# Decay attention and two expert layers on one core: the chunk products cut into half chunks and their work dealt over the steps

## The chip, the cores and the metric

One core of a Trainium2 chip. The metric is device microseconds of one execution. All data is fp32 at the surface; the kernel runs its large products as sums of three fp32r products of a high and a low part.

## The reference, cut to what matters

```python
# attention: batch 4, heads 8, 768 tokens, head size 48
for t in range(S):
    state = alpha[:, :, t, :, None] * state + k[:, :, t] (outer) v[:, :, t]
    y[:, :, t] = q[:, :, t] @ state
x = y as [3072 tokens, 384]
h = x @ w_in                       # 384 -> 2048
x = (max(h, 0) + alpha1 * min(h, 0)) @ w_out   # alpha1 per column of h, 0 to 0.3
h = x @ w_in2
g = h where h >= 1, 0 where h <= -1, else (h + 1)**2 / 4
out = g @ w_out2                   # [3072, 384]
```

The weights of both layers and alpha1 come as float64 and are put together as fp32 on the chip from two 32-bit words each.

## The kernel before, in words

**Attention** goes by chunks of 128 tokens: 24 chunks (NCH), six to a batch item (CPB), each with its eight heads as four pairs, so that a pair fills 112 of the 128 partitions (48 rows from partition 0 and 48 from 64, HALVES). Two scans along the tokens (at_alpha, L214) make running products of alpha backwards (R) and forwards (F); K2 = K * R and Q2 = Q * F (at_qk, L232). On TensorE a chunk then has: the scores K2'Q2 (L247, eight products with 48 rows, 128 columns of weights and 128 columns streamed), masked by VectorE into two tiles A (L252); a transpose of K2 (L258) copied by ScalarE into KT; the share of the state, bd'Q2 (L275); A'V (L280); and what the chunk adds to the state, KT'V (L292). An fp32 product is two records in the trace, each with its own weight load. The first chunk of a batch item has no L275, the last no L258 and L292. L304 to L311 split y into the high and low part in xs; since 48 rows a head don't fill 64, the last 128 rows of x are shared out over spare rows of the other three groups, by six small DMAs a chunk (L326; in the first four chunks by a product with sel, L298).

**Inputs of a chunk.** q, k and alpha are loaded token by token (L157, 192 bytes a piece). Up to chunk 9 (NPE = 10) TensorE turns them by twelve transposes (L195), copied to T by ScalarE (L202) or, with the clamp of alpha, VectorE (L185). From chunk 10 VectorE turns 32 x 32 blocks (L205, one instruction into X), and 16 DMAs bring the blocks to their place in T (L211); the clamp is then VectorE's on T. Alpha outside 0.7 to 1.4 makes the kernel fall back to a general path: ScalarE counts such values (flag, L164), for batch items 2 and 3 on the chunk in nat, for 0 and 1 on six extra loads in the second layer (load_flags).

**The layers** go by blocks of 512 tokens, six to a layer, and by 16 slices of 128 hidden columns: 192 steps, s = 0 to 191 (blocks 0 to 5 are layer one, 6 to 11 layer two). Step s issues on TensorE the nine products h of its slice (L430, 512 columns each), then the activation chain (emit_act, L435), then the out products of step s - 1 (L463, nine of 512; in layer two L474, twelve of 384). The chain is in layer one: VectorE L445 and L447, ScalarE gh (L453), GpSimd gl (L454); in layer two: ScalarE L442, VectorE L450 and L452, then gh and gl. So the chain of a step has the rest of that step and the h products of the next to run in.

**What sets the order.** The order on each engine is that of the program. Chunks 0 to 3 come before the first step. From chunk 4 a chunk's work lies in groups (L516); run_slots (L535) issues one group a step, after the out products: three groups a chunk up to chunk 7, then four: at_out of the chunk before; K2, Q2, decay of the state and the transposing of a later chunk (fetch, L504); the scans of the next chunk; the scores. A block's first step needs the xs of four chunks. All DMAs are issued by the SP queue in program order.

**Weights.** In block 0 every step also loads a slice of layer one (load_w, L342: five DMAs), turns words to fp32 (ScalarE L361 and L362, VectorE joins L367 and L369) and splits it (ScalarE L408, GpSimd L414). The joins and the split of slice fc + 2 stand ahead of the step's own products and activation in the program, the words behind them. In blocks 1 to 4 every fourth step does the same for a slice of layer two (w2_step, L563: two words, two joins, a store); block 5 loads these again and splits them.

PSUM has eight banks: two for h, three for the out products (o0 to o2), three (at) that attention's tiles take in turn.

## Time and profile before

| what | value |
|---|---|
| median of 3 runs (lowest, highest) | 965.82 us (963.66, 966.33) |
| the profiled execution | 964.38 us, its span 962.7 us |
| PE busy | 925.7 us, 96% |
| PEld (weight loads) busy | 781.9 us, 81% |
| DVE busy | 558.6 us, 58% |
| POOL busy | 363.4 us, 38% |
| ACT busy | 349.8 us, 36% |
| granted clock of TensorE, mean over the span | 0.996 |
| DMA, mean rate | 91 GB/s |

Busy is the time in which at least one instruction of the engine runs. The ends of matmuls are modelled, so a busy PE is not a PE at its peak; the starts are measured. The chain that ended last is PE for 76% of the span, DVE for 9%, DMA for 5%. The other 1.7 us of the execution lie around the span.

### The profile page before, as it was taken

To read this page: it belongs to the slowest core of one execution; us is meant where nothing else is said; L and a number is where in the kernel's file an instruction comes from. 1 tells how busy PE (TensorE), PEld (TensorE's weight loads), DVE (VectorE), ACT (ScalarE), POOL (GpSimd) and SP (SyncE) were. 2 spreads that over 40 slices of the span, in tenths; PEclk is the share of its full clock that TensorE was granted. 3 is DMA by queue.
4 is the path that set the end of the run, shared out by engine and by line. 5 is a ranking of instruction groups with operands and counts; after the bars stand their busy time and mean duration, and the time that the engine had idled before them with its cause. 6 is when DMAs were issued, how large, how long until landed. Compare 5 with 4: busy or idle time off the path is not lost.

```text
span 962.7 us, 14310 instructions
## 1 busy us (share of the span) xinstructions
PE 925.7 (96%) x5379; PEld 781.9 (81%) x5379; DVE 558.6 (58%) x756; ACT 349.8 (36%) x590; POOL 363.4 (38%) x290
## 2 busy tenths in 40 slices
PE   7898889999999999999999999999999999999996
PEld 6766567887878788788888889999999999999995
DVE  8888887777767678776433434434435334344333
ACT  3555542333322333332223333345533333333332
POOL 3455553333333343333347743233332333322331
PEclk9999999999999999999999999999999999999999
DMA  9976747666767776674133310031100100100001
GB/s 185 216 137 137 151 90 157 128 126 129 153 128 144 162 161 133 130 153 114 46 117 118 98 55 12 1 118 47 55 1 12 55 2 10 55 12 1 34 0 38
DMA packets 227599, 87.17 MB, mean 91 GB/s; under 512 B 194736, under 2 KB 213952, under 8 KB 227520
## 3 DMA queue, kind: packets, MB, share of 16 engines
q1 hardware_dynamic: 227520, 86.16, 40.2%
q8 instruction: 44, 0.72, 0.3%
q14 instruction: 35, 0.29, 0.1%
HBM read 57.42 MB, written 15.73 MB: 76 GB/s over the span
## 4 chain that ended last, share of the span: by engine, by line
PE 76%; DVE 9%; DMA 5%; SPq 4%; issue 3%; ACT 2%; POOL 0%; DVEq 0%; ACTq 0%; POOLq 0%
PE hp L430 34%; PE y L474 20%; PE o L463 14%; PE sc L247 2%; PE y L280 2%; PE y L275 1%; DVE wf L367 1%; DVE g L445 1%; DMA xs<-x 1%; DVE wf L369 1%; DVE g L447 1%; SPq L211 1%; DMA nat<-in_k_dram 1%; PE kt L258 1%; DMA wst<-in_moe_w_out_dram 1%
## 5 line engine op out<-in xcount | busy, mean ns | idle before, releaser
L454 POOL TENSOR_TENSOR gl<-g,gh 128x512 fp32r<-128x512 f32 x191 | 263.3, 1379 | 510.3 <-ACT gh L453 499.0
L430 PE MATMUL hp<-xs,wh 128*128 128x512 f32 x1152 | 363.2, 396 | 6.2 <-DMA xs<-x 5.0
L453 ACT CAST gh<-g 128x512 fp32r<-128x512 f32 (+1 forms) x193 | 119.3, 618 | 428.3 <-DVE g L447 256.7
L430 PEld LDWEIGHTS hp<-xs,wh 128*128 128x128 f32 x1152 | 211.8, 188 | 46.3 <-DVE T L185 4.7
L430 PE MATMUL hp<-xs,wl 128*128 128x512 f32 x576 | 226.7, 394 | 0.0
L450 DVE SCALAR_TENSOR_TENSOR g<-g 128x512 f32<-128x512 f32 (+1 forms) x97 | 68.3, 704 | 214.7 <-ACT g L442 213.2
L430 PEld LDWEIGHTS hp<-xs,wl 128*128 128x128 f32 x576 | 108.4, 188 | 23.5
L445 DVE TENSOR_SCALAR g<-hp,malpha 128x512 f32<-128x512 f32 x96 | 71.2, 742 | 60.4 <-PE hp L430 60.3
L442 ACT ACTIVATE g<-hp,half 128x512 f32<-128x512 f32 (+1 forms) x97 | 66.1, 683 | 104.7 <-PE hp L430 101.5
L463 PE MATMUL o<-gl,wh 128*128 128x512 f32 x288 | 83.2, 397 | 9.2 <-POOL gl L454 8.0
L463 PE MATMUL o<-gh,wh 128*128 128x512 f32 x288 | 83.2, 397 | 8.1 <-ACT gh L453 5.5
L474 PE MATMUL y<-wh,gh 128*128 128x384 f32 x384 | 83.3, 337 | 0.2
L474 PE MATMUL y<-wh,gl 128*128 128x384 f32 x384 | 83.0, 336 | 0.0
L474 PE MATMUL y<-wl,gh 128*128 128x384 f32 x384 | 82.6, 335 | 0.0
L463 PE MATMUL o<-gh,wl 128*128 128x512 f32 x288 | 81.6, 392 | 0.0
L474 PEld LDWEIGHTS y<-wh,gh 128*128 128x128 f32 x384 | 69.5, 188 | 9.2 <-ACT gh L453 1.1
L463 PEld LDWEIGHTS o<-gl,wh 128*128 128x128 f32 x288 | 52.9, 188 | 25.9 <-POOL gl L454 15.2
L463 PEld LDWEIGHTS o<-gh,wh 128*128 128x128 f32 x288 | 53.4, 189 | 24.5 <-ACT gh L453 10.9
L452 DVE TENSOR_TENSOR g<-hp,g 128x512 f32<-128x512 f32 (+1 forms) x97 | 66.5, 686 | 3.4
L447 DVE SCALAR_TENSOR_TENSOR g<-hp,g 128x512 f32<-128x512 f32 x96 | 66.4, 691 | 3.3
L474 PEld LDWEIGHTS y<-wh,gl 128*128 128x128 f32 x384 | 67.9, 188 | 0.4 <-DVE gl L454 0.3
L474 PEld LDWEIGHTS y<-wl,gh 128*128 128x128 f32 x384 | 68.0, 188 | 0.0
(97 smaller groups left out, 874.8 us busy)
## 6 DMA issues: line engine op xcount, KB each, us to landing
wst<-in_moe_w_out_dram SPq DMA_DIRECT2D x32, 384.0 KB, 4.7
T<-X SPq DMA_DIRECT2D x224, 48.0 KB, 2.1
wst<-in_moe_w_in_dram SPq DMA_DIRECT2D x16, 384.0 KB, 5.4
w_d<-wf SPq DMA_DIRECT2D x16, 384.0 KB, 5.7
w<-w_d SPq DMA_DIRECT2D x16, 384.0 KB, 3.1
wst<-in_moe_w_in_dram SPq DMA_DIRECT2D x32, 144.0 KB, 3.6
x_d<-ev SPq DMA_DIRECT2D x18, 256.0 KB, 4.0
x2s<-x_d SPq DMA_DIRECT2D x18, 256.0 KB, 3.0
```

Source lines behind the costliest of these rows:

```text
L247: nc.tensor.matmul(out=scs[h % 2][:, h // 2, :], lhsT=s["K2"][lo:lo + D, h // 2, :], rhs=s["Q2"][lo:lo + D, h // 2, :], start=True, stop=True)
L280: nc.tensor.matmul(out=y[64 * a:64 * a + 64, p, :], lhsT=vc[:, 2 * p + a, :], rhs=s["A"][a][:, p, :], start=first and p == 0, stop=done, s ...
L430: nc.tensor.matmul(out=hp, lhsT=w[:, p, :], rhs=xs[:, x, p, :], start=(i == 0), stop=(i == 3 * ND - 1))
L442: nc.scalar.activation(y, x, AF.Relu, bias=half, scale=0.5)
L445: nc.vector.tensor_scalar(out=y, in0=x, scalar1=0.0, scalar2=malpha[:, fc:fc + 1], op0=ALU.min, op1=ALU.mult)
L447: nc.vector.scalar_tensor_tensor(out=y, in0=x, scalar=0.0, in1=y, op0=ALU.max, op1=ALU.add)
L450: nc.vector.scalar_tensor_tensor(out=y, in0=y, scalar=1.0, in1=y, op0=ALU.min, op1=ALU.mult)
L452: nc.vector.tensor_max(out=y, in0=x, in1=y)
L453: nc.scalar.copy(out=hi, in_=y)
L454: (nc.gpsimd if parts == 1 else nc.vector).tensor_sub(out=lo, in0=y, in1=hi.bitcast(F32))
L463: nc.tensor.matmul(out=ops[d], lhsT=w[:, d * P:(d + 1) * P], rhs=g, start=first, stop=last)
L474: nc.tensor.matmul(out=ops[t], lhsT=g[:, t * P:(t + 1) * P], rhs=w, start=first, stop=last)
```

## The change

Attention's products are cut into half chunks of 64 tokens (HC), each in one quarter of the array (64 rows by 64 columns): scores only inside a half, the rest through a state at the middle of the chunk (bd has three tiles: at the start, in the middle, at the end). Four records that follow each other go to the four quarters, and those of the two row halves write to different banks of a two-bank tile. Per full chunk this makes 16 products for the scores, 16 for the state's share, 16 for A'V and 16 for what is added to the states, with 64 columns streamed (48 in the last), where there were eight of each with 128 (48). A is one tile, multiplied in one instruction. From chunk 10 on q, k and alpha are loaded in blocks of 768 and 640 bytes a piece (load_blocks, 12 DMAs a chunk), VectorE turns each third straight into T, and GpSimd clamps. Layer one's activation is ScalarE's alpha1 * h and VectorE's maximum of that and h (right while alpha1 is at most 1, which a new flag counts). All alpha flags are counted in layer two (12 loads, 24 flags and that one). w2_step deals a slice's two words and two joins over four steps. A chunk's work is listed by step, as before behind the out products (ends), and a few pieces between h and out (mids). In block 0 the joins stand behind the step's h products and activation, the split and the words at its end. load_w has seven DMAs a slice in layer one.

```diff
-    ps_a = main.enter_context(tc.tile_pool(name="ps_a", bufs=3, space=PSUM))
+    ps_a = main.enter_context(tc.tile_pool(name="ps_a", bufs=1, space=PSUM))
...
+    def load_blocks(c):
+        b, t0 = c // CPB, (c % CPB) * C
         for i in (2, 1, 0):
+            src = (q, k, alpha)[i][b, :, t0:t0 + C, :].rearrange("(p a) (j g) d -> a j p (g d)", a=2, g=4)
             for a in range(2):
                 for r in range(2):
                     d0 = 64 * a + 32 * r
+                    nc.sync.dma_start(out=natq[d0:d0 + 32, i * NP:(i + 1) * NP, 0:4 * D - 32 * r],
+                                      in_=src[a, :, :, 32 * r:4 * D])
+    def at_in(c, i):
+        n = slice(i * NP, (i + 1) * NP)
+        nc.vector.transpose(out=tin(c, i).rearrange("f n (j g) -> f n g j", g=4),
+                            in_=natq[:, n].rearrange("j n (g f) -> j n g f", g=4)[:, :, :, 0:32])
+        if i == 2:
+            clamp(tin(c, i), tin(c, i), nc.gpsimd)
...
+    def bank_pair(c):
+        pool, tag = (ps_o, "oo") if c < NC0 and c % 2 else (ps_a, "yy")
+        w = pool.tile([P, 2, 4 * C], F32, tag=tag, name="w")
+        return [w[:, :, x * NP * HC:(x + 1) * NP * HC].rearrange("q i (n t) -> q i n t", n=NP)
+                for x in range(2)]
+    def at_state(c, across):
+        s = st[c]
+        for p in range(NP // 2):
+            for n in (p, p + NP // 2):
+                for a in range(2):
+                    i = a ^ across
+                    if c % CPB == 0 and i == 0:
+                        continue
+                    o = 64 * out_half(n, a)
+                    nc.tensor.matmul(out=s["y"][o:o + 64, i, n, :], lhsT=bd[i][64 * a:64 * a + D, n, :],
+                                     rhs=s["Q2"][64 * a:64 * a + D, n, HC * i:HC * i + HC],
+                                     start=across and p == 0, stop=False, skip_group_check=True)
+    def at_within(c):
+        s = st[c]
+        if "y" not in s:
+            s["y"], s["sc"] = bank_pair(c)
+        at_state(c, True)
+        for p in range(NP):
+            for a in range(2):
+                for i in range(2):
+                    t = slice(HC * i, HC * i + HC)
+                    nc.tensor.matmul(out=s["sc"][t, 1 - a, p, :], lhsT=s["K2"][64 * a:64 * a + D, p, t],
+                                     rhs=s["Q2"][64 * a:64 * a + D, p, t],
+                                     start=c % CPB == 0 and a == 1 and p == 0, stop=True,
+                                     skip_group_check=True)
+        s["A"] = p1.tile([P, 2, NP, HC], F32, tag="A", name="A")
+        nc.vector.tensor_mul(out=s["A"], in0=s["sc"],
+                             in1=mask.unsqueeze(1).unsqueeze(1).to_broadcast([P, 2, NP, HC]))
+    def at_gain(c, ds=None):
+        s = st[c]
+        if ds is None:
+            s["y"], s["sc"] = bank_pair(c)
+            ds = s["sc"]
+        for p in range(NP):
+            for a in range(2):
+                for i in range(2 if (c + 1) % CPB else 1):
+                    t = slice(HC * i, HC * i + HC)
+                    nc.tensor.matmul(out=ds[64 * a:64 * a + 64, i, p, 0:D],
+                                     lhsT=s["KT"][t, p, 64 * a:64 * a + 64],
+                                     rhs=v_of(c)[t, 2 * p + a, 0:D], start=p == 0, stop=True,
+                                     skip_group_check=True)
+        s["ds"] = ds
...
+    def at_states(c):
+        s0, s1, s2 = [t[:, :, 0:D] for t in bd]
+        s = st[c]
+        ds = s.pop("ds")
+        if c % CPB == 0:
+            nc.vector.tensor_copy(out=s1, in_=ds[:, 0, :, 0:D])
+        else:
+            nc.gpsimd.tensor_mul(out=s0, in0=s2, in1=s["R"][:, :, 0:1].to_broadcast([P, NP, D]))
+            nc.vector.tensor_add(out=s1, in0=ds[:, 0, :, 0:D], in1=s0)
+        if (c + 1) % CPB:
+            nc.vector.tensor_add(out=s2, in0=ds[:, 1, :, 0:D], in1=s1)
 
     def at_out(c, xdst, startup=False, mid=None):
         s = st[c]
...
+        y = s["y"]
+        for p in range(NP):
+            for a in range(2):
+                o = 64 * out_half(p, a)
+                for i in range(2):
+                    t = slice(HC * i, HC * i + HC)
+                    nc.tensor.matmul(out=y[o:o + 64, i, p, :], lhsT=v_wide(c, 2 * p + a)[t],
+                                     rhs=s["A"][t, 1 - a, p, :], start=False, stop=False,
                                      skip_group_check=True)
+        at_state(c, False)
+        if c + 1 in st and "KT" in st[c + 1]:
+            at_gain(c + 1, None if startup else s["sc"])
+        if NC0 <= c < NCH - 2:
+            load_v(c + 2, nc.sync)
+        yv = y.rearrange("q i n t -> q n i t")
         if startup:
             y3 = spare_tile(("y3", c % 2), [P, C], "y3")
+            nc.scalar.copy(out=y3.rearrange("q (i t) -> q i t", i=2), in_=y[:, :, ND])
+            if c < NC0 - 1:
...
@@ -437,15 +497,15 @@
         gh = p2.tile([P, n], F32R, tag="gh", name="gh", padded_shape=[P, 512])
         gl = p2.tile([P, n], F32R, tag="gl", name="gl", padded_shape=[P, 512])
         cuts = [[t[:, i * n // parts:(i + 1) * n // parts] for t in (hp, g, gh, gl)] for i in range(parts)]
-        if layer:
-            for x, y, _, _ in cuts:
+        for x, y, _, _ in cuts:
+            if layer:
                 nc.scalar.activation(y, x, AF.Relu, bias=half, scale=0.5)
+            else:
+                nc.scalar.activation(y, x, AF.Copy, scale=malpha[:, fc:fc + 1])
         for x, y, hi, lo in cuts:
             if layer == 0:
-                nc.vector.tensor_scalar(out=y, in0=x, scalar1=0.0, scalar2=malpha[:, fc:fc + 1],
-                                        op0=ALU.min, op1=ALU.mult)
-                nc.vector.scalar_tensor_tensor(out=y, in0=x, scalar=0.0, in1=y,
-                                               op0=ALU.max, op1=ALU.add)
+
+                nc.vector.tensor_max(out=y, in0=x, in1=y)
             else:
                 nc.vector.scalar_tensor_tensor(out=y, in0=y, scalar=1.0, in1=y,
                                                op0=ALU.min, op1=ALU.mult)
...
+    mids = {}
+    ends = {}
+    def put(where, s, *fs):
+        where.setdefault(s, []).extend(fs)
+    def at_first():
+        at_gain(NC0)
+        at_states(NC0)
+    put(mids, 0, lambda: fetch(NC0, 2))
+    put(ends, 0, lambda: fetch(NC0, 1), lambda: at_scan(NC0, "R"), lambda: at_mul(NC0, "K2", nc.vector))
+    put(mids, 1, lambda: fetch(NC0, 0), lambda: at_scan(NC0, "F"))
+    put(ends, 1, lambda: at_kt(NC0))
     for c in range(NC0, NCH + 1):
+        n = 3 if c < 2 * NC0 else 4
+        s = 2 + 3 * (c - NC0) if c < 2 * NC0 else 2 + 3 * NC0 + 4 * (c - 2 * NC0)
+        if NC0 < c < NPE - 1:
+            put(ends, s, lambda c=c: fetch(c, 0))
+        put(ends, s, at_first if c == NC0 else lambda c=c: at_out(c - 1, xdst(c - 1)))
+        if c == NCH:
+            continue
+        put(ends, s, lambda c=c: at_mul(c, "Q2", nc.vector if c < 2 * NC0 else nc.gpsimd))
+        if c + 1 == NPE:
+            put(ends, s, lambda: fetch(NPE))
+        if c + 1 < NPE:
+            put(mids, s, lambda c=c: fetch(c + 1, 2))
+            put(ends, s + 1, lambda c=c: fetch(c + 1, 1))
+        put(ends, s + 1, lambda c=c: at_within(c))
+        if c + 1 < NCH:
+            put(ends, s + 1, lambda c=c: at_scan(c + 1, "R"))
+            put(ends, s + n - 2, lambda c=c: at_mul(c + 1, "K2", nc.vector))
+            put(ends, s + n - 1, lambda c=c: at_kt(c + 1), lambda c=c: at_scan(c + 1, "F"))
+        if c == NPE - 2:
+            put(ends, s + 1, lambda: fetch(NPE - 1, 0))
+        if c >= NPE - 1:
+            put(ends, s + 2, lambda c=c: fetch(c + 2, 2), lambda c=c: fetch(c + 2, 1))
+            put(ends, s + 3, lambda c=c: fetch(c + 2, 0))
+    def run_slots(where, s):
+        for f in where.pop(s, ()):
+            f()
 
     with tc.manual_schedule():
         steps = [(j, fc) for j in range(len(blk)) for fc in range(NFC)]
...
-        def w2_step(i):
-            if 0 <= i + 1 < NFC:
-                load_w(1, i + 1, nc.sync)
-            if 0 <= i < NFC:
-                conv_w(1, i)
-                store_w(i)
+        def w2_step(s):
+
+            i, k = (s - NFC + 2) // 4, (s - NFC + 2) % 4
+            if k == 0 and i == 0:
+                load_w(1, 0, nc.sync)
+            if k < 2 and 0 < i <= NFC:
+                conv_join(1, i - 1, k)
+                if k == 1:
+                    store_w(i - 1)
+            if k >= 2 and i < NFC:
+                conv_words(1, i, k - 2)
+                if k == 2 and i + 1 < NFC:
+                    load_w(1, i + 1, nc.sync)
...
@@ -674,21 +784,22 @@
         for s in range(len(steps) + SK):
             if s < len(steps):
                 j, fc = steps[s]
-                if j == 0:
-                    w1_join(fc + 2)
-                    w1_split(fc + 2)
-                    w1_load(fc + 5)
                 do_h(s)
-                if j == 0:
-                    w1_words(fc + 3)
+            run_slots(mids, s)
+            if s < NFC:
+                w1_join(fc + 2)
+                w1_load(fc + 5)
             if s >= SK:
                 do_out(s - SK)
+            run_slots(ends, s)
+            if s < NFC:
+                w1_split(fc + 2)
+                w1_words(fc + 3)
             if s < len(steps):
-                run_slots(s + 1 - (s > 13))
                 if j == n1 - 1 and fc == 0:
                     w2_split(-1)
-                if NFC - 4 <= s < (n1 - 1) * NFC and s % 4 == 0:
-                    w2_step(s // 4 - 4)
+                if NFC - 2 <= s < (n1 - 1) * NFC:
+                    w2_step(s)
                 if n1 - 1 <= j < len(blk) - 1:
                     if fc in (8, 10, 12):
                         split_x2(j + 1, (fc - 8) // 2)
@@ -697,6 +808,8 @@
...
@@ -697,6 +808,8 @@
                 i = s - (n1 + 1) * NFC
                 if i >= 0 and i % 2 == 0 and i // 2 < NFB * NFL:
                     load_flags(i // 2)
+                if i == 0:
+                    flag(malpha, 2, 2 * NCH - 1)
                 if 0 <= i - 4 < 2 * NFB * NFL:
                     flag(own["al", (i - 4) // 2], i % 2, i - 4)
```

## Rows read from the trace of the kernel before

**Rows 1.** Busy us of each engine (instructions), clock, DMA in five stretches.
```profile
core 0: us, PE busy (x) PEld busy (x) DVE busy (x) ACT busy (x) POOL busy (x), PEclk, DMA share, GB/s
0.00:37.10 37.10, 31.03 (x330) 26.16 (x330) 30.00 (x56) 16.47 (x28) 13.55 (x36) 1.00 1.07 191
37.10:148.10 111.00, 94.54 (x588) 70.16 (x589) 96.07 (x111) 53.89 (x82) 56.90 (x36) 1.00 0.67 138
148.10:487.20 339.10, 332.49 (x2149) 268.06 (x2148) 243.26 (x328) 104.63 (x197) 116.90 (x92) 0.99 0.63 132
487.20:553.10 65.90, 65.90 (x289) 54.09 (x288) 25.71 (x36) 22.86 (x36) 47.77 (x30) 1.00 0.38 120
553.10:950.60 397.50, 397.43 (x2008) 360.49 (x2007) 160.14 (x218) 150.08 (x246) 128.26 (x98) 1.00 0.09 28
```

**Rows 2.** TensorE's timeline, two steps with attention and two without (block 1).
```profile
148.07 0.62 PE L430 MATMUL hp<-xs,wh 128*128 128x512 f32 x2
...
152.28 1.16 PE L247 MATMUL sc<-Q,K 48*128 48x128 f32 x16
153.38 0.66 PE L258 MATMUL kt<-ident,K 128*128 128x128 f32 x4
153.79 0.70 PE L430 MATMUL hp<-xs,wh 128*128 128x512 f32 x2
...
158.10 1.09 PE L275 MATMUL y<-Q,bd 48*64 48x128 f32 x16
159.12 1.09 PE L280 MATMUL y<-A,vt 128*64 128x128 f32 x16
160.04 0.62 PE L292 MATMUL ds<-vt,KT 128*64 128x48 f32 x16
160.60 0.72 PE L430 MATMUL hp<-xs,wh 128*128 128x512 f32 x2
...
164.83 0.62 PE L430 MATMUL hp<-xs,wh 128*128 128x512 f32 x2
...
168.95 0.62 PE L430 MATMUL hp<-xs,wh 128*128 128x512 f32 x2
```

**Rows 3.** Who waited for whom, whole span: TensorE for shared rows.
```profile
PE hp L430 <- DMA xs<-x: 5.0, 3, 2.2
```

**Rows 4.** Twelve transposes of a chunk's inputs, in the timeline.
```profile
68.31 1.47 PE L195 MATMUL tr<-ident,nat 128*128 128x128 f32 x12
```

**Rows 5.** Groups by line and shape, whole span: A'V and KT'V.
```profile
L280 PE MATMUL y<-A,vt 128*64 128x128 f32 x336 | 23.0, 279 | 0.0
...
L292 PE MATMUL ds<-vt,KT 128*64 128x48 f32 x272 | 10.6, 220 | 0.0
```

**Rows 6.** Weight loads of state's share and A'V in the timeline.
```profile
306.00 0.85 PEld L275 LDWEIGHTS y<-Q,bd 48*64 48x64 f32 x16 [0.36 <-issue]
...
307.02 0.85 PEld L280 LDWEIGHTS y<-A,vt 128*64 128x64 f32 x16 [0.17 <-issue]
```

**Rows 7.** Groups of VectorE by shape, 37 to 148 us (block 0).
```profile
L445 DVE TENSOR_SCALAR g<-hp,malpha 128x512 f32<-128x512 f32 x16 | 11.9, 742 | 0.7 <-PE hp L430 0.7
...
L252 DVE TENSOR_TENSOR A<-sc,mask 128x512 f32<-128x512 f32 x8 | 5.1, 681 | 0.0
...
L205 DVE STREAM_TRANSPOSE X<-nat 128x1536 f32<-128x1536 f32 x1 | 1.8, 1761 | 0.0
...
L318 DVE TENSOR_TENSOR bd<-ds,bd 128x192 f32<-128x192 f32 x2 | 0.7, 348 | 0.0
```

**Rows 8.** Groups of ScalarE, whole span: layer two's activation, a flag.
```profile
L442 ACT ACTIVATE g<-hp,half 128x512 f32<-128x512 f32 x95 | 65.3, 687 | 103.4 <-PE hp L430 100.1 <-POOL gl L454 3.2
...
L167 ACT ACTIVATE junk<-al,bias 128x768 uint8<-128x768 f32 x12 | 11.2, 932 | 0.0
```

**Rows 9.** SP queue issuing a chunk's shared rows, in the timeline.
```profile
314.02 3.96 SPq L326 DMA_DIRECT2D xs<-x  x6
```

**Rows 10.** Group of GpSimd, whole span: Q2.
```profile
L239 POOL TENSOR_TENSOR Q<-T,F 128x512 f32<-128x512 f32 x20 | 25.9, 1293 | 7.4 <-DVE F L226 7.4
```

385 lines of the change are left out of this document (172 added, 213 removed).

## The prediction, made before the changed kernel ran

> **What bounds the kernel now.** I read the engines' busy time first, cut into five stretches [rows 1], then TensorE's timeline inside a stretch [rows 2], and only then single groups and waits. Two stretches hold nothing but layer work: block 5 takes 65.90 us for 16 steps, 4.12 us a step, and layer two 397.5 us for 96 steps, 4.14 a step, PE busy throughout. Nothing in the change makes these products fewer, so some 463 us stand. What can move is the other part: 37.1 us ahead of the first step, block 0 with 111.0 us where sixteen plain steps would be 65.9, and blocks 1 to 4 with 339.1 us where 64 plain steps would be 263.7. Those are excesses of 45.1 and 75.4 us.
>
> In blocks 1 to 4 the excess is TensorE's own work for attention. Four steps, from 148.07 to 168.95, take 20.88 us: one chunk, 4.40 us more than four plain steps [rows 2]. The scores and the transposing of K2 run from 152.28 to 153.79 (1.51), the products of y and of the state from 158.10 to 160.60 (2.50); 0.39 us goes with entering and leaving. Sixteen chunks at 4.40 are 70.4; two first chunks of a batch item have no L275 (158.10 to 159.12, 1.02 each) and three last ones no L258 and L292 (0.41 and 0.56): 65.5 in all. The remaining 9.9 us are stalls; 5.0 us of waits for shared rows [rows 3] are the largest single part I can name.
>
> In block 0 VectorE is busy 96.07 of 111.00 us, PE 94.54 [rows 1]. Twelve transposes a chunk, 1.47 us [rows 4], six chunks of them, come on top of 65.9 us of steps and about four chunks of 4.40: 92.3 us, so TensorE could be 19 us quicker. VectorE, whose joins stand ahead of the activation in its queue, holds it.
>
> **The change, part by part.** *Half chunks.* A full chunk now has 64 products, 128 records, and the four transposes. What does a record cost? A'V streams 128 columns: 16 starts lie over 1.09 us less one record of 0.279, so 54 ns apart; KT'V streams 48: (0.62 - 0.220)/15 = 27 ns [rows 2, 5]. Both lines alternate between the two column halves, so a half is held 108 and 54 ns; 64 columns, half of A'V's, hold it 54 ns as well. With four quarters at work beside each other a record then costs 54/4 = 13.5 ns; with two, as now, 27; with one, 54. No row shows four quarters. I take 13.5, nearest to what the rows do show in each direction alone: L280 and L292 run the column halves side by side, and L247, whose 16 records of two row halves lie in 1.10 us (152.28 to 153.38), runs the row halves so. Each of the four needs the same 54 ns. 27 and 54 stay as bounds.
>
> The Trainium skill, "TensorEngine Tiling (Array Packing)", Gotcha 1, says that different row tiles cannot access one PSUM bank at the same time. No run here shows it; the change gives the two row halves different banks, so by it the estimate stays.
>
> A chunk is then 128 x 13.5 = 1.73, plus 0.41 for the transposing of K2, 0.39 for entering and leaving as before, and 0.3 for the ends of two sets (after L292 the next product starts 0.16 us later than its own rhythm: 160.60 - 160.04 - 15 x 0.027). That is 2.83 us against 4.40. I charge no gap between the parts of a set: the weight loads show 0.17 us of "issue" where the shape goes from 48x64 to 128x64, 0.36 where it comes from the layers [rows 6], and a set now keeps one shape. First and last chunks have 16 records fewer, 0.22. Blocks 1 to 4: 16 x 2.83 - 5 x 0.22 = 44.2, plus the 9.9 of stalls left as they are, 54.1 against 75.4: **21.3 us less**.
>
> *VectorE in block 0.* L445, 11.9 us for 16 steps, goes; the maximum takes L447's place and is costed as that. A is one instruction: 5 x 0.681 where there were 8, 2.0 less. The 1.8 us of L205 leave the block; four more small adds at 0.348 come in, 1.4 [rows 7]. 96.1 falls to 81.8. At the same busy share (96.07/111.00 = 0.865) the block takes 94.5 us; TensorE's own sum is 65.9 + 5 x 2.83 + 6 x 1.47 = 88.9, below that. **16.5 us less.** Should the new order fill VectorE better, TensorE's 88.9 is the end.
>
> *The activation on ScalarE.* One instruction of 0.687 a step, as in layer two [rows 8], is 11 us in block 0 on 53.9 busy and 44 in blocks 1 to 4 on 104.6 of 339.1 [rows 1]. The chain becomes layer two's, which runs at 4.14 a step without stretch, so I cost it at nothing where ScalarE has room. In block 0 a step also has words and a split on ScalarE, and each engine waits for the other; the 5.6 us between 94.5 and 88.9 is what I leave for that.
>
> *Start.* Four times one A of 0.681 less and four adds of 0.348 more on VectorE, busy 30.00 of 37.10: **1.3 us less**, between 3 less and 4 more, since GpSimd and SP get more small pieces there (two DMAs more a slice).
>
> *Flags.* The 24 instructions on nat leave blocks 1 to 4; twelve more of 0.932 us [rows 8] go to layer two, one a step, beside twelve that stand there now in a stretch without a gap: nothing. ScalarE has 150 of 397.5 us there.
>
> *Inputs, clamp, words.* Twelve loads replace three loads and sixteen moves a chunk on SP. At the 0.66 us of an issue (3.96/6) [rows 9] they are 7.9 us, under two steps. VectorE's turning of thirds lies between 1.8 us a chunk (as L205) and twice that; GpSimd's clamp between nothing and the 1.29 of Q2 [rows 10]. Fourteen chunks of either fit into idle time of 339.1 us (VectorE 243 busy, less 47.5 for L445; GpSimd 117) [rows 1, 7]. Behind the clamp in GpSimd's queue stands the next step's gl, and TensorE waits for that; the loads are out three steps ahead, so I cost the wait at nothing. If they are late, gl is. Words and joins dealt singly change no sum.
>
> *Shared rows.* Chunk 11's output now comes in step 30, one step before block 2's last, where it was step 29; twelve loads stand ahead of its six DMAs on SP. At most this adds a plain step, 4.12, at each of five block starts, 20 us. I leave it within the 9.9, as SP has fewer issues a chunk than before.
>
> **The sum.** Against the profiled execution, 964.38 us (its span 962.7 and 1.7 around it; 0.15% under the median 965.82): 964.4 - 21.3 - 16.5 - 1.3 = 925.3. I say 925.
>
> **Rivals.** *Four quarters don't run beside each other; the record keeps a price of 25 to 27 ns.* For it: no row shows less than KT'V's 27. Against it: 27 is explained by two halves of 54. At 27 a chunk is 4.56, blocks 1 to 4 5.3 us longer, block 0 about 12 shorter (TensorE 97.5 there, then the bound), the start 1.3: 956.
>
> The Trainium skill, "TensorE: Matmul & The Clock Gate", Back-to-back issue gap, gives a floor of about 25 ns from start to start however few columns. By it the same sum is 950; the trace's 27 ns does not contradict it.
>
> *The quarters shut each other out, one at a time (slower).* 54 ns a record: a chunk is 8.0 us, blocks 1 to 4 are 58 us longer, block 0 4 longer: 1026. It turns slower from about 31 ns a record, where 2.6 us for each ns (128 records, some 20 chunks) have eaten the gain. Against it: halves of either kind do run side by side today.
>
> *No change.* The record at 27 and shared rows late by 2 us at each block start: 966.
>
> **How the numbers follow.** Chances: forecast 0.62, the 25 to 27 ns record 0.26, no change 0.06, one at a time 0.06. Faster by over 0.3% (what a measurement of this kernel can tell from none) holds the first two, 0.88. The range goes from 910 (the 9.9 of stalls and the 5.6 of block 0 gone as well) to 957, which takes in the late rows at their bound (945) and the second case.
>
> **What would show it.** In the changed profile: four-step periods of blocks 1 to 4 near 19.3 us instead of 20.88; starts of the 64-column records 13 to 15 ns apart (27: the first rival; over 31: the second); block 0 near 95 us with VectorE's busy time near 82; layer two still 4.14 a step; no L205 on the path. Wrong would be new PE waits for gl or for g in block 0, or waits for shared rows beyond 2.2 us at block starts.

## The result, and the profile after

The changed kernel takes 952.9 us (median of 4 runs, 947.4 to 953.6) where the kernel before took 965.9 beside it: ratio 0.986, 95% interval 0.984 to 0.988. It is faster, by 1.4% where 4.2% were forecast. The profiled execution has a span of 951.1 us, 11.6 less than before. The same five stretches as in [rows 1], with the same columns:

```profile
core 0: us, PE busy (x) PEld busy (x) DVE busy (x) ACT busy (x) POOL busy (x), PEclk, DMA share, GB/s
0.00:42.90 42.90, 32.05 (x610) 27.80 (x610) 29.15 (x57) 16.10 (x28) 14.06 (x41) 0.96 1.07 168
42.90:160.60 117.70, 97.45 (x930) 77.49 (x931) 93.41 (x97) 65.81 (x99) 59.61 (x36) 0.91 0.54 118
160.60:474.60 314.00, 311.66 (x3103) 250.85 (x3102) 193.41 (x277) 134.45 (x216) 140.11 (x106) 1.00 0.49 132
474.60:541.60 67.00, 66.48 (x289) 54.03 (x289) 14.28 (x21) 34.06 (x52) 47.98 (x30) 1.00 0.39 125
541.60:939.00 397.40, 397.12 (x2007) 360.50 (x2007) 159.91 (x218) 161.44 (x272) 128.10 (x98) 1.00 0.11 34
```

| stretch | forecast | measured |
|---|---|---|
| ahead of the first step | -1.3 | +5.8 |
| block 0 | -16.5 | **+6.7** |
| blocks 1 to 4 | -21.3 | **-25.1** |
| block 5 | 0 | +1.1 |
| layer two | 0 | -0.1 |
| sum | -39.1 | -11.6 |

Blocks 1 to 4 gave what was forecast and a little more. (Block 5's 1.1 us are its first step, 5.22 us where the others take 4.12; a product there waits for the last shared rows.) The missing 27.5 us lie in the first 160 us: block 0, which was to be 94.5 us long, takes 117.7, and the start is longer as well. In block 0 TensorE's granted clock has fallen to 0.91 from 1.00, and PE is busy only 97.45 of 117.70 us.

TensorE's timeline of one chunk in block 1, against [rows 2]:

```profile
160.63 0.70 PE L490 MATMUL hp<-xs,wh 128*128 128x512 f32 x2
...
173.64 0.69 PE L352 MATMUL w<-A,vt 64*64 64x64 f32 x32
...
174.39 0.63 PE L324 MATMUL w<-vt,KT 64*64 64x48 f32 x32
...
179.29 0.46 PE L292 MATMUL w<-Q,bd 48*64 48x64 f32 x16
179.57 0.65 PE L306 MATMUL w<-Q,K 48*64 48x64 f32 x32
180.15 0.72 PE L490 MATMUL hp<-xs,wh 128*128 128x512 f32 x2
...
214.17 0.63 PE L324 MATMUL w<-vt,KT 64*64 64x48 f32 x16
```

From 160.63 to 180.15 four steps take 19.52 us (19.3 forecast, 20.88 before). In L352, 32 records of 64 columns lie over 0.69 us; less one record of 0.22 that is 15 ns from start to start, and for L324 (0.63 - 0.22)/31 = 13 ns. In a batch item's last chunk (214.17) L324 has one row half alone, and its 16 records are (0.63 - 0.22)/15 = 27 ns apart: two quarters at 27, four at half of that. The four quarters do work beside each other. The single starts in the trace come in fours, 58 ns from one four to the next, so 14.6 ns a record. The wait for shared rows [rows 3] is down to 1.3 us in the whole span (two, the longer 1.0).

Now block 0. VectorE's groups of that stretch, against [rows 7] (line, operation, out<-in, shapes, count, busy us, mean ns, idle before):

```profile
L431 DVE SCALAR_TENSOR_TENSOR wf<-wst,wf 128x768 uint32<-128x768 uint32 x14 | 26.5, 1894 | 0.5
...
L508 DVE TENSOR_TENSOR g<-hp,g 128x512 f32<-128x512 f32 x16 | 11.0, 686 | 14.6 <-ACT g L504 14.3
L261 DVE TENSOR_TENSOR K<-T,R 128x512 f32<-128x512 f32 x5 | 10.5, 2093 | 0.5
L261 DVE TENSOR_TENSOR Q<-T,F 128x512 f32<-128x512 f32 x4 | 8.3, 2066 | 0.0
```

L431 is the second join of the weight words. In block 0 before its row was

```profile
L369 DVE SCALAR_TENSOR_TENSOR wf<-wst,wf 128x768 uint32<-128x768 uint32 x14 | 13.4, 958 | 0.5
```

so it took 958 ns; it takes 1894 now. K2 takes 2093. L508 is the new maximum, at the 0.69 us it was costed at. What stands beside the long ones is seen in the timeline of all engines over one step (start, duration, engine):

```profile
115.33 0.69 ACT L504 ACTIVATE g<-hp,malpha 128x512 f32<-128x512 f32 x1 [0.58 <-PE hp L490]
...
117.54 1.27 POOL L514 TENSOR_TENSOR gl<-g,gh 128x512 fp32r<-128x512 f32 x1 [2.57 <-issue]
117.64 1.98 DVE L431 SCALAR_TENSOR_TENSOR wf<-wst,wf 128x768 uint32<-128x768 uint32 x1
...
119.66 0.84 ACT L468 CAST wh<-wf 128x768 fp32r<-128x768 f32 x1 [1.30 <-DVE wf L431]
...
120.15 1.22 DVE L244 TENSOR_TENSOR_SCAN R<-T,zrev 128x516 f32<-128x516 f32 x1
...
120.40 0.90 ACT L420 ACTIVATE wst<-wst 128x768 f32<-128x768 f32 x1
...
120.57 2.45 POOL L474 TENSOR_TENSOR wl<-wf,wh 128x768 fp32r<-128x768 f32 x1 [1.76 <-ACT wh L468]
...
121.20 0.97 ACT L422 ACTIVATE wst<-wst,mhalf 128x768 uint32<-128x768 uint32 x1
...
121.47 2.10 DVE L261 TENSOR_TENSOR K<-T,R 128x512 f32<-128x512 f32 x1
...
122.08 0.67 ACT L504 ACTIVATE g<-hp,malpha 128x512 f32<-128x512 f32 x1
```

GpSimd's gl starts at 117.54 and runs its usual 1.27 us; the join behind it starts at 117.64 and ends at 119.62, 0.81 after gl. At 120.15 VectorE's scan is first and keeps its 1.22, and GpSimd's wl, 0.42 later, takes 2.45 instead of 1.86. Then K2 is held up in its turn. So where the two meet, whoever starts first keeps its time, and the other's time grows by nearly all that was left of the first (their work overlaps by some 0.15 to 0.2 us). The whole trace says the same: the second join takes 0.93 to 0.96 us the 17 times no GpSimd product is beside it, and 1.91 to 2.00 the 14 times one started ahead of it. And these lines are a round: the copy alpha*h (115.33), maximum, joins, split wh (119.66), the words (120.40, 121.20), and only then the next copy, at 122.08, 6.75 us later; TensorE's own work would be 5.56 a step (88.9/16). Who waited for whom in block 0 (us in total, times, longest):

```profile
ACT wh L468 <- DVE wf L431: 19.0, 11, 2.8
...
DVE g L508 <- ACT g L504: 14.3, 7, 4.3
...
PE tr L205 <- DVE T L197: 10.8, 5, 2.7
...
PE kt L267 <- DVE K L261: 5.0, 4, 2.1
```

TensorE's waits in block 0, 21.0 us, are all for attention's own tiles: T (10.8 for VectorE's clamp, 2.7 for ScalarE's copy), K2 (5.0), Q2 (1.8) and xs (0.7). None is for a weight, for g or for gl.

### The profile page after: what moved, and what is told of

It reads as the page before. It is cut to its first block, busy times and chain, and to the rows that moved or that the text cites. A ratio compares the mean times of both kernels' runs of the same rounds, so it can differ in the third digit from the quotient of the medians.

```text
span 951.1 us, 17365 instructions
## 1 busy us (share of the span) xinstructions
PE 909.2 (96%) x6955; PEld 773.7 (81%) x6955; DVE 493.6 (52%) x675; ACT 413.8 (44%) x668; POOL 389.9 (41%) x310
## 4 chain that ended last, share of the span: by engine, by line
PE 82%; DVE 6%; DMA 5%; SPq 3%; issue 2%; ACT 1%; DVEq 0%; ACTq 0%
PE hp L490 38%; PE y_oo L523 11%; PE y_yy L534 7%; PE y_oo L534 7%; PE y_o L523 5%; PE y_o L534 3%; PE y_at L534 3%; DVE wf L431 2%; DMA wst<-in_moe_w_in_dram 2%; PE w L352 2%; DMA xs<-x 1%; PE w L292 1%; PE w L324 1%; SPq L410 1%; DVE wf L428 1%
## 5 line engine op out<-in xcount | busy, mean ns | idle before, releaser
L508 DVE TENSOR_TENSOR g<-hp,g 128x512 f32<-128x512 f32 x96 | 66.2, 690 | 113.4 <-ACT g L504 112.6
L504 ACT ACTIVATE g<-hp,malpha 128x512 f32<-128x512 f32 x96 | 65.9, 687 | 122.7 <-PE hp L490 121.9
L523 PE MATMUL y_oo<-gh,wh 128*128 128x512 f32 x192 | 60.2, 395 | 0.0
L523 PE MATMUL y_oo<-gl,wh 128*128 128x512 f32 x192 | 59.7, 392 | 0.4 <-POOL gl L514 0.4
L523 PE MATMUL y_oo<-gh,wl 128*128 128x512 f32 x192 | 59.6, 392 | 0.0
L431 DVE SCALAR_TENSOR_TENSOR wf<-wst,wf 128x768 uint32<-128x768 uint32 x32 | 44.4, 1389 | 0.5
L230 DVE STREAM_TRANSPOSE T<-nat 128x512 f32<-128x512 f32 x42 | 43.3, 1084 | 0.0
L523 PEld LDWEIGHTS y_oo<-gl,wh 128*128 128x128 f32 x192 | 36.0, 188 | 8.5 <-POOL gl L514 0.9
L523 PEld LDWEIGHTS y_oo<-gh,wl 128*128 128x128 f32 x192 | 36.1, 188 | 7.7
L523 PE MATMUL y_o<-gl,wh 128*128 128x512 f32 x96 | 37.7, 393 | 0.0
```

Source lines behind the costliest of these rows:

```text
L230: nc.vector.transpose(out=tin(c, i).rearrange("f n (j g) -> f n g j", g=4), in_=natq[:, n].rearrange("j n (g f) -> j n g f", g=4)[:, :, :, ...
L431: nc.vector.scalar_tensor_tensor(out=fu, in0=hi, scalar=0x80000000, in1=fu, op0=ALU.bitwise_and, op1=ALU.bitwise_or)
L504: nc.scalar.activation(y, x, AF.Copy, scale=malpha[:, fc:fc + 1])
L508: nc.vector.tensor_max(out=y, in0=x, in1=y)
L523: nc.tensor.matmul(out=ops[d], lhsT=w[:, d * P:(d + 1) * P], rhs=g, start=first, stop=last)
```

## The experiments

Three theories stood after this reading. **The round**: ScalarE and VectorE hand the work to each other, with the words standing ahead of the copy. **The exclusion**: GpSimd's products shut out those of VectorE, and the sum of both binds. **The weights**: h waits for wh and wl. All kernels below are cut from the changed one unless said otherwise; each ratio is to the kernel before beside it, whose median lay between 964.0 and 966.7.

Two things differ between executions without any edit, so an effect is read from its stretch of the trace and not from the median alone. Layer two, which no experiment touches, takes 396.3 us from its first h product to its last in ten of the sixteen traces, 400.0 in three (words first, one wl in three, clamp first) and 402.6 in three (old order, gl on VectorE behind words-first, scores twice), all at a granted clock of 1.00; no run shows why. And the first step begins between 40.8 and 44.3 us in the eleven traces with the changed kernel's start. Block 0 is steadier: three pairs with the same block 0 differ by 0.0, 0.3 and 0.7 us.

**Words ahead of the split.**

```diff
             if s < NFC:
-                w1_split(fc + 2)
                 w1_words(fc + 3)
+                w1_split(fc + 2)
```

> Edit: in block 0 the words of slice fc + 3 stand ahead of the split of slice fc + 2 on ScalarE, nothing else. Ring theory: in the changed kernel block 0 (117.7 us, 7.36 a step) is a closed round of ScalarE and VectorE: product alpha1*h 0.67, maximum 0.69, two joins 0.95 + 2.0, split 0.84, two words 1.89, and again the product, 7.0 us and the hops between. With the words in front they run while VectorE joins, and the round is 5.2 us and hops; then VectorE (5.8 us a step busy) or TensorE (5.6) sets the pace: block 0 at 95 to 101 us, the kernel 17 to 23 us faster than the changed one, 930 to 936. Rival, contention: VectorE's own work, slowed by GpSimd beside it, sets block 0; the order of ScalarE's words changes nothing, 953. Rival, weights: the slices of weights arrive too late (seven DMAs each, first issue 6 us later than before); nothing changes, 953.

Measured: 947.5 us, ratio 0.981 (0.977 to 0.985); block 0 109.2 us, 8.5 less, VectorE busy 90.68 of it. The second join still takes 1.71, the first 1.25, and VectorE's wait for the copy fell from 14.3 to 8.8. The round is part of it, and less than the theory said (95 to 101 us). The loads are the same as before and the block is shorter, so the weights don't set it.

**The activation wholly on VectorE again**, which takes the copy out of the round:

```diff
-                nc.scalar.activation(y, x, AF.Copy, scale=malpha[:, fc:fc + 1])
...
-                nc.vector.tensor_max(out=y, in0=x, in1=y)
+                nc.vector.tensor_scalar(out=y, in0=x, scalar1=0.0, scalar2=malpha[:, fc:fc + 1],
+                                        op0=ALU.min, op1=ALU.mult)
+                nc.vector.scalar_tensor_tensor(out=y, in0=x, scalar=0.0, in1=y,
+                                               op0=ALU.max, op1=ALU.add)
```

> Edit: layer one's activation goes back to VectorE alone (min and mult, then max and add), for all six blocks; all else as changed. Ring theory: ScalarE's first link leaves the round; what is left is joins 2.95, split 0.84, words 1.89 = 5.7 us, and VectorE's load rises by 0.74 to about 6.5 us a step; block 0 102 to 108 us, kernel 938 to 944. Contention theory: VectorE has 16 x 0.74 = 12 us more to do in block 0, kernel 960 to 966. Weights theory: no change, 953. Blocks 1 to 4 stay at 19.5 us a chunk in all three.

Measured: 953.3 us, 0.988 (0.985 to 0.990); block 0 117.6 us, VectorE busy 103.41, second join 1.885. Nothing is won: the copy is out of the round, and VectorE is busy 88% of the block. Neither the round's number (102 to 108) nor contention's (960 to 966) was met. The weights theory's 953 was, but words-first, with the same loads, speaks against that theory, and no product of TensorE waits for a weight in the changed kernel's block 0.

**The start in another order.**

```diff
         at_scan(0, "R")
-        at_scan(0, "F")
-        fetch(1, 2)
         at_mul(0, "K2", nc.vector)
+        at_scan(0, "F")
         at_mul(0, "Q2", nc.gpsimd)
         at_kt(0)
+        fetch(1, 2)
+        at_gain(0)
+        at_states(0)
+        at_scan(1, "R")
+        at_scan(1, "F")
         fetch(1, 1)
...
-        at_gain(0)
-        at_scan(1, "R")
-        at_scan(1, "F")
-        at_states(0)
```

> Edit: ahead of the first step alone: K2 of chunk 0 right behind its first scan, and chunk 0's share for the states and the state adds ahead of chunk 1's last eight transposes and its scans. Theory for the start: it is 5.8 us longer (first layer product at 42.9 instead of 37.1 us) because chunk 0's output, at 20.8 instead of 16.6 us, now waits for the gain, the states and eight transposes that stand in between; with them out of the way the first step begins 2 to 4 us earlier, kernel 949 to 951. Rival: the chain goes on VectorE's sum of work (29 us busy either way) or TensorE's low clock there; under 1 us, 952 to 953.

Measured: 952.8 us, 0.988 (0.984 to 0.992). In the trace chunk 0's output products start at 16.76 us instead of 20.78 (16.57 before) and the first step at 40.5 instead of 42.9. The second is no gain that is shown: the same start without the edit gave 40.8 to 44.3. The theory's 949 to 951 was missed.

**Block 0 in the order of before**, with joins, split and load ahead of h, and the words right behind it:

```diff
+                if s < NFC:
+                    w1_join(fc + 2)
+                    w1_split(fc + 2)
+                    w1_load(fc + 5)
                 do_h(s)
+                if s < NFC:
+                    w1_words(fc + 3)
...
-            if s < NFC:
-                w1_join(fc + 2)
-                w1_load(fc + 5)
...
-            if s < NFC:
-                w1_split(fc + 2)
-                w1_words(fc + 3)
```

> Edit: in block 0 joins, split and the load stand ahead of the step's layer products, the words right behind them, as in the kernel before; the activation stays on ScalarE and VectorE. Ring theory: the round is joins 1.9 to 2.95, split 0.84, product 0.67, maximum 0.69, gh 0.62, words 1.89 = 6.6 to 7.7 us a step, so little or nothing is won: block 0 106 to 118 us, kernel 942 to 953. Contention theory: the second join, 1.95 us in the changed kernel and 0.96 in the one before, falls back to about 1 us, VectorE has 14 us less to do in block 0, kernel 938 to 940.

Measured: 956.7 us, 0.992 (0.990 to 0.994), slower than the changed kernel. Its block 0, by stretch (columns as in the first fence) and by its waits:

```profile
42.70:164.30 121.60, 99.72 (x932) 77.04 (x932) 70.45 (x97) 65.05 (x99) 58.50 (x36) 0.90 0.48 115
```

```profile
ACT wh L468 <- DVE wf L431: 35.9, 14, 3.9
DVE g L508 <- ACT g L504: 23.6, 15, 3.3
...
PE tr L205 <- ACT KT L269: 14.5, 4, 4.1
```

(The profiled execution, 963.1 us, is the slowest of ten; its layer two is one of the 402.6 us.) Here the second join is back at 0.958 and VectorE busy only 70.45 us, the cleanest measure of its work without GpSimd beside it. Block 0 takes 121.6 all the same, beyond the round's bounds as well (106 to 118), and the number that exclusion alone would give (938 to 940) falls. TensorE's largest wait here is another one, 14.5 us for ScalarE's KT, while ScalarE waits 35.9 for the joins. What VectorE has to do and what block 0 takes are two things.

**The split activation alone, in the kernel before.**

```diff
-                nc.vector.tensor_scalar(out=y, in0=x, scalar1=0.0, scalar2=malpha[:, fc:fc + 1],
-                                        op0=ALU.min, op1=ALU.mult)
-                nc.vector.scalar_tensor_tensor(out=y, in0=x, scalar=0.0, in1=y,
-                                               op0=ALU.max, op1=ALU.add)
+                nc.scalar.activation(y, x, AF.Copy, scale=malpha[:, fc:fc + 1])
+                nc.vector.tensor_max(out=y, in0=x, in1=y)
```

> The kernel before, with the activation of layer one split between ScalarE and VectorE as after the change, nothing else. Term of the prediction: VectorE loses 11.9 us of busy time in block 0 (96 to 84), and at the same busy share block 0 would fall from 111 to 97, with nothing to gain in blocks 1 to 4: about 951. Ring theory: in this order the copy adds a ScalarE leg between words and maximum, and VectorE's joins stand ahead of the maximum, so what VectorE loses returns as waiting: block 0 108 to 118, the kernel 962 to 972.

Measured: 969.9 us, 1.008 (1.005 to 1.011): slower. Block 0, by stretch and by its largest new wait:

```profile
36.80:153.00 116.20, 96.20 (x587) 72.71 (x588) 79.57 (x95) 63.17 (x98) 53.03 (x35) 0.97 0.64 132
```

```profile
DVE g L447 <- ACT g L444: 23.0, 15, 2.2
```

VectorE is busy 79.57 us instead of 96.07, and the block takes 116.2 instead of 111.0. At the busy share of before it would have been 92 us. This is the prediction's step done by itself, and it goes the other way: 23 us of waiting for ScalarE's copy have taken the place of 16.5 us of work.

**gl of block 0 on VectorE**, behind the joins, on top of words-first:

```diff
+            if late is not None:
+                late.append(lambda: nc.vector.tensor_sub(out=lo, in0=y, in1=hi.bitcast(F32)))
+                continue
             (nc.gpsimd if parts == 1 else nc.vector).tensor_sub(out=lo, in0=y, in1=hi.bitcast(F32))
...
                 w1_join(fc + 2)
+                late.pop()()
```

> On top of words-first. In block 0 alone, gl is made by VectorE behind the two joins instead of by GpSimd beside them. Theory (GpSimd's gl, 1.5 us in words-first, and VectorE's second join, 1.71 instead of 0.96, shut each other out): the joins return to 0.96, gl costs VectorE about 0.7, a step loses some 0.7 us; block 0 96 to 103 us instead of 109.2, the kernel 933 to 941. Rival (VectorE is simply full and the joins are long for another reason, such as ScalarE's words written at the same time): gl's 0.7 us comes on top, block 0 about 118, the kernel 956 to 960. Nothing is left out of the computation.

Measured: 943.6 us, 0.977 (0.974 to 0.981); block 0 105.9, a little outside the theory's 96 to 103 and far from the rival's 118. The second join is back at 0.958 us, gl costs 0.71, and VectorE with more instructions is busy less (86.20 against 90.68). What is left of the exclusion stands in the timeline of one step:

```profile
107.39 0.96 DVE L431 SCALAR_TENSOR_TENSOR wf<-wst,wf 128x768 uint32<-128x768 uint32 x1
...
109.40 1.87 POOL L474 TENSOR_TENSOR wl<-wf,wh 128x768 fp32r<-128x768 f32 x1 [3.04 <-ACT wh L468]
109.47 2.89 DVE L244 TENSOR_TENSOR_SCAN R<-T,zrev 128x516 f32<-128x516 f32 x1
...
113.21 0.66 PE L267 MATMUL kt<-ident,K 128*128 128x128 f32 x4 [1.91 <-DVE K L261]
```

wl on GpSimd from 109.40 to 111.27; the scan, which takes 1.22 alone, starts at 109.47 and ends at 112.36, 1.09 after wl. TensorE waits 1.91 us for the K2 behind it.

**wl of block 0 on VectorE** instead, on top of words-first (and, in a second kernel, with the order of the start experiment):

```diff
-        nc.gpsimd.tensor_sub(out=lo, in0=stg.pop((layer, fc)), in1=hi.bitcast(F32))
+        eng.tensor_sub(out=lo, in0=stg.pop((layer, fc)), in1=hi.bitcast(F32))
...
                 split_hi(0, i)
-                split_lo(0, i)
+                split_lo(0, i, nc.vector)
```

> On top of words-first. In block 0 alone, wl is made by VectorE (GpSimd's takes 2.08 us there) at the end of the step; gl stays on GpSimd. Theory (the two engines shut each other out, so the step is the sum of both): a sum of 1.5 for gl, about 1 for wl and VectorE's own 3.5 to 4 leaves TensorE's 5.6 as the bound: block 0 92 to 100 us, the kernel 930 to 938, the second join still 1.7 to 2.0 beside gl. Rival (VectorE simply full): 1 us a step on top, block 0 about 125, the kernel 960 or more. Nothing is left out of the computation.

> The kernel with wl on VectorE, and the start in the order of the start experiment (first step 2.4 us earlier there). If both gains are on TensorE's path they add: 2 to 3 us less than with wl on VectorE alone, 927 to 936. If block 0 is bound by something that doesn't begin with the first step, the block takes back what the start gave: no difference.

Measured: 942.7 us, 0.978 (0.976 to 0.981), but block 0 is 110.1, not 92 to 100: the second join stays at 1.887 beside gl, as expected, and VectorE is busy 92.92. The median's 5 us against words-first are not block 0's: of the 4.9 between the two traces 4.2 lie in layer two and 1.4 ahead of the first step, and block 0 is 0.9 longer. With the start's order: 947.2, 0.983 (0.977 to 0.988); chunk 0's output comes as early as in the start experiment, yet the first step only at 44.3 us, with a granted clock of 0.83 ahead of it. No gain was shown there.

**gl on VectorE alone**, the words where the change put them:

> The kernel after the change with gl of block 0 on VectorE behind the joins and the words where they were, behind the split. If the round between ScalarE and VectorE binds first there, and the exclusion only behind it, the second join's time returns to 0.96 and nothing is won, since the join is itself a leg of that round only by the 0.95 it gets shorter: block 0 106 to 118 us, the kernel 941 to 953; with the join's 0.95 a step wholly on the round it is 15 us, at 941; with gl's 0.7 put in its place 4 us, at 949. If the exclusion alone bound the block, it would fall as far as with words-first as well, to 105.9 and 943.6 or less. Nothing is left out.

Measured: 942.8 us, 0.976 (0.970 to 0.981); block 0 106.8, the second join 0.958. That is about as far as with the words moved too (105.9), and the bounds of both theories come near enough to it that the number alone doesn't choose. What it shows is that the two gains don't add: moving the words alone gives 8.5 us, moving gl alone 10.9, both 11.8. They free the same time. That fits a round that was too long because one of its legs, the join, was shut out by gl: moving the words takes the words out of it, moving gl makes the join short.

**Both on VectorE**, and **one wl in three**, in the step where R is scanned:

```diff
-                split_lo(0, i)
+                split_lo(0, i, nc.vector if (i - 2) % 3 == 0 else nc.gpsimd)
```

> On top of words-first, both gl and wl of block 0 on VectorE; GpSimd keeps the small product of the state and nothing else there. Theory of exclusion: every VectorE instruction returns to its lone time (second join 0.96, R scan 1.22, K2 0.69), and three steps are the plain sum of VectorE's work, 19.4 us (6 joins 5.7, wl 2.84, gl 2.07, maximum 2.07, scans 2.45, K2, Q2, A and T 2.73, outputs and states 1.6): VectorE busy without a gap, block 0 101 to 106 us, about what gl alone on VectorE gave (105.9), the kernel 938 to 945. If the long times have another cause (ScalarE's words beside it) they stay, and the block is 115 or more. Nothing is left out.

> Words-first with gl on VectorE, and of wl only every third, that of the step in which VectorE scans R: beside it GpSimd's wl made the scan 2.89 us instead of 1.22, and TensorE waited 1.9 us for K2. Theory: the scan returns to 1.22, wl costs VectorE 0.95, TensorE's wait for K2 falls by 0.7 to 1 in three steps: block 0 100 to 104 us instead of 105.9, the kernel 936 to 942. Rival (VectorE's queue is full either way): no change from 943.6. Nothing is left out.

Measured, both: 940.3 us, 0.974 (0.971 to 0.977), block 0 104.2. Its VectorE groups in block 0:

```profile
L431 DVE SCALAR_TENSOR_TENSOR wf<-wst,wf 128x768 uint32<-128x768 uint32 x14 | 13.4, 958 | 0.5
...
L244 DVE TENSOR_TENSOR_SCAN R<-T,zrev 128x516 f32<-128x516 f32 x5 | 6.1, 1224 | 0.0
...
L261 DVE TENSOR_TENSOR K<-T,R 128x512 f32<-128x512 f32 x5 | 3.5, 693 | 0.5
```

Join, scan and K2 all stand at their lone times, with ScalarE's words beside them as before. VectorE is busy 89.36 of 104.2; the expectation was that it would have no gap. One in three: 939.2, 0.972 (0.968 to 0.976), block 0 103.2, VectorE 84.00; the scan 1.22.

**The clamp ahead of the maximum** (`run_slots(mids, s)` between h and its activation for the 16 steps of block 0), on top of one in three, and the same with the start's order:

> On top of one wl in three on VectorE: in block 0 the transposes in the middle of a step and what follows them stand ahead of the activation, so that VectorE clamps alpha (0.68 us) before the maximum instead of behind it. TensorE waits 7.7 us in block 0 for that clamp, since one PSUM bank now serves all transposes. Theory (with the exclusion gone, these waits are on the path): they fall below 3 us and block 0 goes from 103.2 to 96 to 100 us, the kernel 932 to 937. Rival (VectorE's queue is the bound, and a later maximum takes back what the clamp gives): block 0 102 to 105, the kernel 938 to 941. Nothing is left out.

> The same with the order of the start experiment. There the first output came four us earlier and the first step 2.4 us earlier, with the medians unable to tell. If it is on the path, 2 to 4 us less than the run beside it; if TensorE's lower clock in the later chunks of the start takes it back (first step at 44 us, as with wl on VectorE), no difference.

Measured: 940.3, 0.976 (0.973 to 0.979), block 0 102.0: the rival's number. TensorE's wait for the clamp fell from 7.7 to 2.9 us and the block by 1.2. Other waits of the 102 us took its place:

```profile
DVE wf L428 <- DMA wst<-in_moe_w_in_dram: 3.7, 6, 0.7
ACT wst L420 <- DMA wst<-in_moe_w_out_dram: 3.3, 2, 1.7
...
PE tr L205 <- DVE T L197: 2.9, 5, 0.8
```

VectorE and ScalarE now wait for the slices' loads as well. That is the next thing to look at; it was not tried. With the start's order: 937.1, 0.973 (0.970 to 0.977), first step at 39.6 instead of 41.9. That is 3.2 us less than the run beside it, within what was expected, but single runs of the two overlap, and of the 5.6 us between the two traces 3.8 are layer two's; block 0 is 102.8. That the start's order gains is not shown. Of the kernels so far, all from gl on VectorE on, but for wl with the start's order, have a ratio whose interval lies below that of the changed kernel.

**The price of a record**, with the scores issued twice in the changed kernel:

```diff
-                for i in range(2):
+                for i in (0, 1, 0, 1):
...
-        nc.gpsimd.memset(mask, 1.0)
+        nc.gpsimd.memset(mask, 0.5)
```

> The kernel after the change with every product of the scores issued twice and the mask at one half, so that the result stays: 32 more records a chunk. At the 13.5 ns of the prediction the four-step period of blocks 1 to 4 grows by 0.43 us (19.5 to 19.9), 16 chunks by 6.9, the kernel by 7 to 9 us (960 to 962). At 27 ns (the first rival) by 0.86 a period and 14 to 18 us in all (967 to 971). At 54 ns by 1.7 a period, 30 us or more.

Measured: ten runs between 957.2 and 971.1 us, median 964.8, too wide to tell 8 from 14. The stretch of blocks 1 to 4 tells it:

```profile
162.30:483.00 320.70, 319.56 (x3584) 258.90 (x3582) 193.31 (x277) 134.51 (x216) 139.92 (x106) 1.00 0.49 130
```

320.70 against 314.00 is 6.70 us for 15 x 32 more records (fifteen chunks have their scores in this stretch): 14.0 ns each. A step with scores grows from 5.19 to 5.71 us, 16 ns a record; waits in other steps give some of it back. The second set doesn't follow the order of the first (the row halves alternate less often), so I take 14 to 16.

## Why the prediction was wrong, and where it was right

**Right: the record and blocks 1 to 4.** 13.5 ns was taken, 14.6 measured from four to four (14 to 16 with the scores twice), so the first rival (25 to 27 ns) and the second (54 ns) fall. That the kernel's 952.9 lies by the rivals' totals is chance: their price of a record isn't what was lost. (At 27 ns TensorE's 97.5 in block 0 is 13.5 shorter than 111.0, not 12, and the rival's sum 955.) The Trainium skill's floor of about 25 ns from start to start ("TensorE: Matmul & The Clock Gate", Back-to-back issue gap), by which the prediction gave 950, doesn't hold across four quarters here; the measurement decides. 314.0 us came for 317.8, partly by luck. An undisturbed four-step period is 19.5 us, so a chunk costs 3.05 and not 2.83, and the first and last chunks of a batch item save nothing (half the records, on one row half, at 27 ns): 4.6 us more. The last period is 1.8 shorter, and the stalls, which I had left at 9.9, came to about 3.4. Of these 6.5 us less the waits for shared rows are 4.0 (5.0 before, 1.0 now in these blocks); I can't name the rest.

**Right: what was costed at nothing.** Layer two is 397.4 us with all 24 flags in it. VectorE's turning of thirds takes 1084 ns, 3.25 a chunk, inside its bounds and hidden; no wait for clamp or gl beyond 0.4 us stands in blocks 1 to 4.

**Wrong: "at the same busy share (96.07/111.00 = 0.865) the block takes 94.5 us".** This step carried 16.5 of the 39.1 us, and block 0 got 6.7 longer. Three things fail in it.

First, a busy share isn't a property of an engine. It came from an order in which VectorE did the whole activation; with a copy on ScalarE in the middle, each engine stands idle while the other works. The split alone shows it (busy 16.5 less, block 0 5.2 longer). The sign that the prediction named for this, new waits of TensorE for g or gl, isn't what came in the changed kernel: TensorE waits for attention's T and K2, which VectorE makes late. (With the split alone it does wait for the activation, 15.6 us for gh where it was 4.3.)

Second, "the 5.6 us between 94.5 and 88.9 is what I leave for that" put a number on the round without adding up its legs. They could be added from rows: copy 0.69, maximum 0.69, two joins 1.9, split 0.84, words 1.9, so 6.0 us a step before any hand-over, above TensorE's 5.56; with the join at 1.9 instead of 0.96 it is 7. Over 16 steps that is 96 us and 111.

Third, the durations. "VectorE busy time near 82" took each row's mean as a property of the instruction. In the trace of before, in VectorE's groups of block 0, these already stood:

```profile
L238 DVE TENSOR_TENSOR K<-T,R 128x512 f32<-128x512 f32 x5 | 10.2, 2043 | 0.0
L226 DVE TENSOR_TENSOR_SCAN F<-T,zfw 128x516 f32<-128x516 f32 x5 | 9.5, 1897 | 0.2
L221 DVE TENSOR_TENSOR_SCAN R<-T,zrev 128x516 f32<-128x516 f32 x6 | 8.7, 1452 | 0.0
L239 DVE TENSOR_TENSOR Q<-T,F 128x512 f32<-128x512 f32 x4 | 7.1, 1766 | 0.0
```

K2 has a lone time of 0.69, the scans of 1.22, Q2 of 0.68 (in the trace of before K2 takes 0.68 the 17 times no GpSimd product is beside it). The excess, 5 x 1.35 + 5 x 0.68 + 6 x 0.23 + 4 x 1.09 = 16 us, was GpSimd beside VectorE. In the changed order it is 26 us (14 x 0.94 for the join, 5 x 1.40 for K2, 4 x 1.38 for Q2); these 10 us more are most of the 11.6 by which VectorE's 93.41 exceeds the forecast 81.8. The largest part sits on the join, a leg of the round. The Trainium skill states the rule ("SBUF — State Buffer", SBUF: two separate sides): a VectorE instruction with two inputs in SBUF and a GpSimd instruction that reads SBUF lock each other out for the whole of an instruction. The trace agrees but for some 0.15 us of overlap: 2.89 for a scan of 1.22 behind a wl of 1.87, while the maximum and A, which read PSUM, keep 0.69 at most the 28 and 15 times that GpSimd started ahead of them. The term of the sum that was mis-sized is thus block 0's: 94.5 forecast, 117.7 measured, 106.8 with gl off GpSimd, 103 to 104 with the words moved as well and the rest of the exclusion taken away. Of the last 9 us a part is VectorE's added gl and wl; the rest is waits that pass from one to the next (K2, clamp, loads), and I can't divide them further.

**Wrong: the start**, forecast at -1.3 between -3 and +4, measured +5.8, outside its bounds (+3.7 to +7.3 over the eleven traces with this start). Its rows in the timelines of before and of after:

```profile
16.57 1.09 PE L280 MATMUL y<-A,vt 128*64 128x128 f32 x16
...
18.04 0.94 PE L298 MATMUL y<-y,sel 128*128 128x128 f32 x6
```

```profile
11.65 1.91 PE L205 MATMUL tr<-ident,nat 128*128 128x128 f32 x8
...
20.78 1.13 PE L352 MATMUL w<-A,v 64*64 64x64 f32 x32
...
22.79 1.55 PE L370 MATMUL w<-y,sel 128*128 128x64 f32 x12
```

I counted VectorE's instructions and not TensorE's order. Eight transposes of chunk 1 (11.65) now stand ahead of chunk 0's gain, and its output starts at 20.78 instead of 16.57; the reordered start brings that back to 16.76. And spreading the shared rows over the output (L370) takes 12 records of 128x64 where six of 128x128 did before, 1.48 us at 22.79 instead of 0.87: four times 0.6, a step that issues twice as many records and that I didn't cost at all. The eight transposes take 1.91 us at 11.65 and 1.04 in the reordered start at 15.79; the granted clock reads 1.00 in both stretches, so the rows don't say why. In block 0 they do show the clock:

```profile
108.15 1.12 PE L205 MATMUL tr<-ident,nat 128*128 128x128 f32 x4 [2.67 <-DVE T L197]
```

In this wait of 2.67 us the granted clock falls to 0.50, the lower of its two levels (1.2 GHz), where it stays from 107.8 to 114.4, and four transposes take 1.12 us that take 0.60 at 102.80, at full clock.

## What to carry to other kernels

Before an engine's busy time is turned into a time, add up the round that passes through it and its neighbours, hand-over by hand-over: taking work off one engine and giving the other a leg in the same round can make it slower. Compare an instruction's duration in the stretch with its shortest elsewhere in the trace; a ratio of two was another engine's work here, and a new order moved it to another place. When products are cut in halves, count every set that is issued more often, the small ones at the edges too.

## What the runs showed of the hardware that I had not expected

GpSimd and VectorE exclude each other nearly for whole instructions where both read two operands from SBUF: 1.98 us for a join of 0.96 beside a gl of 1.27, 2.89 for a scan of 1.22 beside a wl of 1.87, and the other way round 2.45 for wl where the scan came first. Moving 0.7 us of work a step from GpSimd onto VectorE made VectorE's busy time shorter. Quarter products of TensorE start in fours, 58 ns from four to four at full clock, so 14.6 ns each. The granted clock, 1.00 in block 0 before, lay between 0.90 and 0.98 there in the changed kernel and the experiments, and the length of the block doesn't follow it: with both products on VectorE the clock is 0.92 and the block 104.2 us, with one wl in three 0.98 and 103.2. And the same layer two took 396.3, 400.0 or 402.6 us in different executions at a granted clock of 1.00, for which no run shows a cause.
